# Strassen's seven products for the first channel product of the last two batches

## The chip, the cores and the metric

The kernel runs on one core of a Trainium2 chip, in one launch. The metric is the time of one execution in microseconds, as the median of several runs. The core has five engines that each take their instructions in order: PE (TensorE, matmuls and weight loads), DVE (VectorE), ACT (ScalarE), POOL (GpSimd, here the issuer of most loads) and SP (SyncE, the issuer of stores and of transposing DMAs). They wait for each other through semaphores.

## The reference

Attention with a squared ReLU in place of softmax, for 8 batches, 12 heads, 448 positions and 64 values a head, and a mixer layer on its result:

```python
scores = (q @ k.transpose(0, 1, 3, 2)) / sqrt(64)
attn = maximum(scores, 0) ** 2 / 448
x = (attn @ v).transpose(0, 2, 1, 3).reshape(8, 448, 768)
h = maximum(x.transpose(0, 2, 1) @ w_tok1, 0) @ w_tok2      # 448 -> 256 -> 448, over positions
u = x + h.transpose(0, 2, 1)
out = u + maximum(u @ w_ch1, 0) @ w_ch2                     # 768 -> 1536 -> 768, over channels
```

Inputs and output are float32; the kernel multiplies in bfloat16 and accumulates in float32.

## The kernel before, in words

The work is cut into 24 super-steps `s` of four heads, three to a batch. For each there are, by the names that stand in the code and in the order:

- `ld{k,q,v}{s}.{half}`: loads, cast to bfloat16 on the way, issued by POOL (L274). `kqT` is then made either by PE (`T{s}`, L379, with the copies `cp`, for the first ten super-steps) or by a transposing DMA: VectorE copies `k` and `q` into the one buffer `side` (`ik`, `iq`, L398), SP issues the transpose (`xk`, `xq`, L402).
- `S{s}.{c}`, seven score products (L420), each four matmuls of 64 rows and 64 columns that share the array; `r{s}.{c}.{e}`, their two evictions with the ReLU (L252 on ScalarE or L254 on VectorE), into one of ten buffers `sq`; `q{s}.{c}`, the square, on VectorE (L427).
- `V{s}.{c}`, the products with `v` (L444), again 64 x 64; `xe`, their evictions (L454, L456); `X`/`xc` or `xd`, the transpose of the result, by PE or by DMA (L467).
- `t1`, `rt`, `t2`, `u`: the token products (L488, L497) and the addition of `x` into `uT` (L501). `ub{b}.{g}` transposes `uT` back to `u_sb` by DMA (L513).

For each batch `b` there are twelve chunks of the first channel product, `C1.{b}.{e}` (L533): six matmuls of 128 x 128 weights from `wc1` and 448 columns of `uT`, accumulated in one PSUM bank and evicted with the ReLU to `r2` by `c1e{b}.{e}`. `r2` and `u_sb` are rings of eleven blocks of 128 rows.

The second channel product already goes by Strassen's seven products, over pairs `p` of row blocks: `P1.{p}` to `P7.{p}` (L584), six matmuls each, on weights summed once at the start (`ws`, L317) and on sums of `r2` (`s1` to `s4`, L571). Products that enter two outputs are accumulated in one bank and read out in between: `a`, `b`, `c` and `f21` (L599) add `u_sb` and write an output block, `f11`, `f12`, `f22` (L601) add to what is there. `st` are the stores (L633).

The order of all engines is one list, `ORDER`, written out in the file: each word is an operation, with the PSUM banks for a PE operation (`S0.2:23`) and the engine for an eviction (`:A` ScalarE, `:D` VectorE). `fill:2*13` is 13 matmuls with no use but to keep PE running. An engine executes its operations in the list's order; there is no scheduler behind it.

`ident`, the unit matrix for PE's transposes, is made by POOL. It stands behind nine loads in POOL's queue.

Of the kernel before, what the change touches and what calls it, by code (L numbers as in the profile page):

```python
# [6 lines left out]
FP32 = mybir.dt.float32  # L7
# [8 lines left out]
NSUM = 6  # L16

# [43 lines left out]
ldf.1 ldk0.0 ldf.0 ldk0.1 ldq3.1 ldk2.1 ldq1.0 ldq1.1 cast1.0:A cast1.1:D ldk1.0 ldk1.1 ldv0.1 cast0.0:D cast0.1:A  # L61
ident ldv0.0 T0.0:0 T0.1:1 ldq2.0 cp0.0:A cp0.1:D ldk2.0 fill:2*13 S0.2:23 ldq2.1 S0.5:45 S0.3:67 r0.2.0:A r0.2.1:D
S0.4:10 ldv1.1 r0.3.1:A r0.5.0:D r0.3.0:A ldk3.0 r0.5.1:D T1.0:23 r0.4.1:A ldq3.0 q0.2:D S0.1:74 r0.4.0:A ldv1.0
cp1.1:D cp1.0:A r0.1.0:D ldv2.1 r0.1.1:A fill:5*19 S1.1:65 q0.3:D ldq4.1 S0.0:01 S1.0:32 r1.1.1:A S1.2:74 q0.1:D
r0.0.0:A ldk3.1 r0.0.1:D r1.2.1:A ldv2.0 r1.2.0:D r1.0.1:A r1.0.0:A q0.0:D wc1.0 r1.1.0:A q0.4:D V0.0:50 S1.3:14
wt1.1 q0.5:D V0.1 r1.3.0:A V0.2 r1.3.1:D S1.6:72 wt1.0 V0.3 S0.6:36 q1.0:D V0.4 r1.6.1:A ldk4.0 r0.6.1:D V0.5
r0.6.0:A T2.0:14 ldq4.0 r1.6.0:A q1.1:D cp2.1:A ldk4.1 cp2.0:D q0.6:D wt2 q1.2:D fill:2*24 V0.6 S1.5:26 S1.4:37
q1.3:D ldv3.1 xe0.0:A S2.4:14 r1.5.0:A r1.5.1:D xe0.1:A r1.4.1:D r1.4.0:A X0.1:5 q1.5:D V1.0:26 xc0.1:A S2.2:07
q1.4:D V1.1 r2.2.1:A r2.2.0:D V1.2 T3.0:35 r2.4.0:A q1.6:D r2.4.1:A S2.1:70 V1.3 cp3.0:D cp3.1:A V1.4 r2.1.1:D V1.5
r2.1.0:A q2.2:D V1.6 S2.0:14 S2.5:35 xe1.0:A q2.1:D S3.2:07 r2.0.0:A r2.0.1:D r2.5.0:A ldv3.0 r2.5.1:D xe1.1:A  # L70
q2.0:D r3.2.0:A ldk6.1 r3.2.1:A q2.4:D V2.0:21 S2.3:43 S3.1:56 q2.5:D V2.1 r2.3.1:A ldv4.1 S2.6:07 r2.3.0:D V2.2
r3.1.0:A ldk5.0 r2.6.1:D r2.6.0:A S3.5:34 X1.1:5 r3.1.1:A q2.3:D ldk5.1 r3.5.1:A q2.6:D ldq6.0 fill:0*9 V2.3
r3.5.0:A S3.0:07 xc1.1:D S3.4:64 V2.4 r3.0.0:A r3.0.1:D X1.0:3 ldk6.0 r3.4.1:A X0.0:5 q3.1:D V2.5 xc1.0:A S3.3:07
ldq5.0 xc0.0:D V2.6 r3.4.0:A q3.0:D t1.0.1:4 ldq5.1 xe2.0:A xe2.1:D T4.0:35 rt0.1:A ldv4.0 r3.3.1:D r3.3.0:A X2.0:6
X2.1:2 cp4.1:A q3.2:D t1.0.0:1 ldv5.0 t1.1.0:4 cp4.0:D rt0.0:A ldq6.1 t1.1.1:0 xc2.0:A xc2.1:D rt1.0:D S3.6:75 wc1.1
# [631 lines left out]
```

## Time and profile before

| | |
|---|---|
| median of 3 runs | 364.04 us (363.62 to 365.6) |
| the profiled execution | 361.52 us |
| its span, first to last instruction | 359.7 us |
| PE busy | 342.2 us, 95% |
| VectorE busy | 296.4 us, 82% |
| ScalarE busy | 192.4 us, 53% |
| POOL busy | 92.1 us, 26% |
| granted TensorE clock | 0.994 |

Times in the profile are microseconds from the first instruction of one profiled execution. A busy PE is not PE at its peak, since a matmul's record holds its latency and matmuls overlap: rates are read from the length of a run of matmuls. A group's line gives the count, the busy time, the mean of one in ns, and the idle time ahead of them with what ended it.

### The profile page before, as it was taken

What the parts mean: (1) busy time and instruction counts of PE and PEld (TensorE: products, weight loads), DVE (VectorE), ACT (ScalarE), POOL (GpSimd) and SP (SyncE); (2) the same over time, 40 slices, a digit from 0 to 9 for tenths busy, and PEclk for the clock granted to TensorE, in tenths of its full rate; (3) what the DMA queues carried; (4) which work ended last, traced back from release to release, by engine and by line L of the source; (5) the groups of instructions that cost most, each with busy time, mean ns of one, the idle gap of its engine ahead of it and who ended that gap; (6) DMA issues with size and microseconds to landing.
All of it is one profiled execution on the core that took longest, in us unless ns stands there. A gap on an engine that the chain in (4) does not pass through costs nothing.

```text
span 359.7 us, 8735 instructions
## 1 busy us (share of the span) xinstructions
PE 342.2 (95%) x3494; PEld 190.6 (53%) x3494; DVE 296.4 (82%) x568; ACT 192.4 (53%) x407; POOL 92.1 (26%) x157
## 2 busy tenths in 40 slices
PE   5787999999999999999999999799999999999994
PEld 3565555455546545555545555355455555555562
DVE  1899999998899998999799999699999954165283
ACT  3789987764862187831776155464777322431300
POOL 8847533056054230640203071110300000000000
PEclk9899999999999999999999999999999999999999
DMA  8999999569999999999699999974794221631435
GB/s 153 168 196 173 156 202 202 102 98 163 169 154 179 143 175 183 175 183 138 95 210 144 172 130 161 236 123 84 122 162 108 56 41 29 157 76 23 104 105 158
DMA packets 100505, 50.42 MB, mean 140 GB/s; under 512 B 72880, under 2 KB 97136, under 8 KB 100464
## 3 DMA queue, kind: packets, MB, share of 16 engines
q0 software_dynamic: 25904, 21.47, 44.1%
q1 hardware_dynamic: 74240, 28.00, 43.4%
q8 instruction: 27, 0.44, 0.5%
q10 hardware_dynamic: 320, 0.39, 0.3%
q14 instruction: 14, 0.11, 0.1%
HBM read 43.38 MB, written 11.01 MB: 151 GB/s over the span
## 4 chain that ended last, share of the span: by engine, by line
PE 80%; DMA 8%; issue 5%; DVE 3%; POOL 3%; DVEq 0%; POOLq 0%
PE m_ps L533 27%; PE m_ps L584 25%; PE sc_ps L420 8%; PE acc_ps L444 8%; PE t_ps L488 6%; PE h_ps L497 5%; DMA kqT<-side 4%; DMA v_raw<-in_v_dram 2%; DMA k_raw<-in_k_dram 2%; POOL k_raw L274 1%; PE kqT_ps L379 1%; DVE sq L427 1%; DVE sq L254 1%; POOL v_raw L274 1%; PE x_ps L479 1%
## 5 line engine op out<-in xcount | busy, mean ns | idle before, releaser
L252 ACT ACTIVATE sq<-sc_ps 128x448 bf16<-128x448 f32 x213 | 102.5, 554 | 38.7 <-PE sc_ps L420 37.5
L533 PE MATMUL m_ps<-uT_sb,wc 128*128 128x448 bf16 x576 | 118.5, 353 | 0.0
L427 DVE TENSOR_TENSOR sq<-sq 128x896 bf16<-128x896 bf16 x168 | 97.2, 619 | 0.2
L252 ACT ACTIVATE r_sb<-m_ps 128x448 bf16<-128x448 f32 (+3 forms) x115 | 51.6, 471 | 70.1 <-PE m_ps L533 69.8
L533 PEld LDWEIGHTS <-wc 128*128 128x128 bf16 x576 | 54.1, 98 | 54.6 <-issue 9.0
L254 DVE TENSOR_SCALAR sq<-sc_ps 128x448 bf16<-128x448 f32 x123 | 71.3, 618 | 6.6 <-PE sc_ps L420 6.4
L444 PE MATMUL acc_ps<-sq,v_raw 64*64 64x448 bf16 x672 | 56.7, 354 | 4.4 <-DVE sq L427 2.4
L420 PE MATMUL sc_ps<-kqT 64*64 64x448 bf16 x672 | 57.9, 356 | 2.8 <-DVE xT L456 1.7
L274 POOL DMA_DIRECT2D v_raw<-in_v_dram x48 | 29.4, 615 | 78.7 <-PE acc_ps L444 62.7
L274 POOL DMA_DIRECT2D k_raw<-in_k_dram x48 | 29.5, 621 | 72.2 <-DVE side L398 44.2
L584 PEld LDWEIGHTS <-r_sb 128*128 128x128 bf16 x336 | 32.5, 98 | 24.0 <-issue 1.6
L599 DVE TENSOR_TENSOR out_sb<-m_ps,u_sb 128x384 f32<-128x384 f32 x56 | 30.8, 553 | 11.7 <-PE m_ps L584 11.3
L420 PEld LDWEIGHTS <-kqT 64*64 64x64 bf16 x672 | 22.9, 106 | 20.4 <-issue 12.9
L584 PEld LDWEIGHTS <-sums 128*128 128x128 bf16 x252 | 24.3, 98 | 17.4 <-issue 0.4
L444 PEld LDWEIGHTS <-v_raw 64*64 64x64 bf16 x672 | 20.5, 106 | 21.7 <-issue 14.4
L274 POOL DMA_DIRECT2D q_raw<-in_q_dram x46 | 28.3, 626 | 11.9 <-DVE side L398 11.2
L584 PE MATMUL m_ps<-wc,r_sb 128*128 128x384 bf16 x168 | 31.3, 326 | 0.0
L501 DVE TENSOR_TENSOR uT_sb<-h_ps,xT 128x448 bf16<-128x448 f32 x48 | 28.8, 617 | 3.0 <-PE h_ps L497 3.0
L584 PE MATMUL m_ps<-wc_t,r_sb 128*128 128x384 bf16 x168 | 30.7, 326 | 0.2 <-DVE out_sb L599 0.2
L584 PE MATMUL m_ps<-wc_t,sums 128*128 128x384 bf16 x168 | 30.8, 326 | 0.0
L601 DVE TENSOR_TENSOR out_sb<-m_ps,out_sb 128x384 f32<-128x384 f32 x42 | 23.0, 553 | 8.4 <-PE m_ps L584 8.1
L252 ACT ACTIVATE r_sb<-t_ps 128x512 bf16<-128x512 f32 (+1 forms) x25 | 13.9, 559 | 26.2 <-PE t_ps L488 26.2
(49 smaller groups left out, 246.6 us busy)
## 6 DMA issues: line engine op xcount, KB each, us to landing
out_dram<-out_sb SPq DMA_DIRECT2D x52, 192.0 KB, 3.1
k_raw<-in_k_dram POOLq DMA_DIRECT2D x48, 112.0 KB, 5.2
v_raw<-in_v_dram POOLq DMA_DIRECT2D x48, 112.0 KB, 5.2
q_raw<-in_q_dram POOLq DMA_DIRECT2D x46, 112.0 KB, 5.1
wc<-in_moe_w_ch_dram POOLq DMA_DIRECT2D x2, 1152.0 KB, 10.6
wc<-in_moe_w_ch_dram POOLq DMA_DIRECT2D x3, 576.0 KB, 9.1
u_sb<-uT_sb SPq DMA_TRANSPOSE x60, 3.2
sums<-in_moe_w_ch_dram POOLq DMA_DIRECT2D x1, 576.0 KB, 14.7
```

Of the source, the lines that this page charges most:

```text
L252: nc.scalar.activation(out, ps, AF.Relu)
L254: nc.vector.tensor_scalar(out=out, in0=ps, scalar1=0.0, scalar2=None, op0=ALU.max)
L274: nc.gpsimd.dma_start(out=raws[t][s % NR[t]][64 * half:64 * (half + 1)], in_=src[b, h0:h0 + 2].rearrange('e (p c) d -> p e (c d)', c=KC))
L420: nc.tensor.matmul(o.ps[e][64 * half:64 * (half + 1), :S], lhsT=lhsT, rhs=rhs, start=True, stop=True, skip_group_check=True)
L427: sq_ops[s, c] = [add(Op(f'q{s}.{c}', 'DVE', lambda o: nc.vector.tensor_tensor(out=buf, in0=buf, in1=buf, op=ALU.mult), ev))]
L444: nc.tensor.matmul(o.ps[half][64 * e:64 * (e + 1), :S], lhsT=r[rows, e, c * D:(c + 1) * D], rhs=sq[rows, e, :], start=c == 0, stop=c == KC ...
L488: nc.tensor.matmul(o.ps[:, j, :], lhsT=wt1[:, c, j * 128:(j + 1) * 128], rhs=x_sb[:, p0:p1, c, :], start=c == 0, stop=c == 3)
L501: nc.vector.tensor_tensor(out=uTs[bb % 2][:, 2 * i + a, off:off + S].rearrange('n (c p) -> n c p', c=KC), in0=t2.ps[:, :S].rearrange('n (p ...
L533: nc.tensor.matmul(ps[:, :S], lhsT=wc1[:, g, e * 128:(e + 1) * 128], rhs=uT[:, g, off:off + S], start=g == 0, stop=g == CC - 1)
L584: nc.tensor.matmul(banks[into][:, :HN], lhsT=lhs[:, e], rhs=wc2[w][:, e], start=after is None and e == 0, stop=e == EH - 1, skip_group_che ...
L599: nc.vector.tensor_tensor(out=out_[:, cols].rearrange('n (g d) -> n g d', d=128), in0=banks[into][:, :HN].rearrange('n (g d) -> n g d', d= ...
L601: nc.vector.tensor_tensor(out=out_[:, cols], in0=banks[into][:, :HN], in1=out_[:, cols], op=ALU.add)
```

## The change

The first channel product of batches 6 and 7 is computed for both together (`PAIRED = 2`). The two batches are the two column halves of one matrix, the two halves of the 768 inputs its row halves, and `wc1` is a 2 x 2 matrix of halves of inputs and outputs. Seven products of half size, `Q1` to `Q7`, for each of six blocks `k` of 128 outputs, three matmuls each, take the place of 2 x 12 chunks of six matmuls. With them come

- `y1` to `y4`, sums of the weights, in two halves each, on VectorE; three of them go to the buffers of `k` and `q` once the last super-steps have left them, one over a quarter of `wc1`;
- `m1` to `m4`, sums of the inputs, in two parts each, on VectorE; they go to `sq` buffers, `m3` over a part of `uT`;
- `na`, `nb`, `nc`: float32 snapshots of the accumulating bank, in `sq` buffers (most on ScalarE);
- `h11`, `h12`, `h22`: VectorE adds a bank and a snapshot into `r2`, without the ReLU; `h21` evicts with the ReLU;
- `g1`, `g2`: the ReLU in place on `r2`.

Batch 6 lies over the end of the ring `r2`, so its writes are two pieces, of 128 and 320 columns. To make the buffers adjacent, the `k` and `q` buffers become one tile, and the `sq` buffers one. The whole of `ORDER` is another list; it also splits evictions between ScalarE and VectorE in other places, loads `wc1` later, and has `ident` behind seven loads instead of nine, and the second half of the first transposes ahead of the first.

```diff
+PAIRED = 2
 ORDER = """
-ldf.1 ldk0.0 ldf.0 ldk0.1 ldq3.1 ldk2.1 ldq1.0 ldq1.1 cast1.0:A cast1.1:D ldk1.0 ldk1.1 ldv0.1 cast0.0:D cast0.1:A
-ident ldv0.0 T0.0:0 T0.1:1 ldq2.0 cp0.0:A cp0.1:D ldk2.0 fill:2*13 S0.2:23 ldq2.1 S0.5:45 S0.3:67 r0.2.0:A r0.2.1:D
...
+ldf.1 ldk0.1 ldf.0 ldk0.0 ldq1.1 ldk1.0 ldk1.1 ldq1.0 cast1.0:A cast1.1:D ldv0.0 ident cast0.0:D cast0.1:A ldv0.1
+T0.1:0 T0.0:1 ldk2.1 cp0.1:A cp0.0:D ldq2.0 fill:2*13 S0.6:23 ldk2.0 S0.4:45 S0.1:67 r0.6.0:A r0.6.1:D S0.0:10
...
+h11.1:D Q7.1 ub6.0 h22.0:D Q5.1:3 g2.0:D na.2:A Q3.0 h11.2:D Q6.2 h12.0:D Q4.0 nb.2:A ub6.4 nc.1:D P5.9:6 g1.0:A
+h21.0:D Q1.3:4 h22.1:D P4.9 f22.9:D na.3:A g2.1:D Q3.1 f21.9:D Q1.4:2 h12.1:D st19.0 Q2.3:1 ub7.4 g1.1:A Q7.2
...
+h12.4:D Q4.4 g1.4:D nc.5:A Q2.5:1 st19.1 h21.4:A h22.5:D P1.10:0 h11.5:D g2.5:A Q3.5 a.10:D Q4.5 h12.5:D P2.10:7
+h21.5:A g1.5:D s1.10:D P1.11:4 s1.11:D s2.10:D P5.10:5 a.11:D s2.11:D P6.10 s3.11:D s3.10:D P6.11 b.10:D s4.10:D
...
 """
...
-    raws = {t: [sbuf.tile([128, 2, KC * D], BF16, name=f'{t}_raw{i}') for i in range(NR[t])] for t in 'kqv'}
+    kq_raw = sbuf.tile([128, NR['k'] + NR['q'], 2, KC * D], BF16, name='kq_raw')
...
-    sqs = [sbuf.tile([128, 2, S], BF16, name=f'sq{i}') for i in range(NSQ)]
+    sq_all = sbuf.tile([128, NSQ, 2, S], BF16, name='sq')
+    sqs = [sq_all[:, i] for i in range(NSQ)]
+    GH = CC // 2
+    spare = kq_raw.rearrange('p i e d -> p (i e d)')[:, :3 * GH * HC].rearrange('p (w g n) -> p w g n', w=3, g=GH)
+    wsq = {1: spare[:, 0], 2: spare[:, 1], 4: spare[:, 2], 3: wc1[:, :GH, HC:]}
...
+    snaps = [sq_all[:, 6 + i].rearrange('p e n -> p (e n)').bitcast(FP32) for i in range(4)]
...
+    def channel1_pair(b):
...
+        B = {(i, j): uT[:, (low, high)[i], j * S:(j + 1) * S] for i in range(2) for j in range(2)}
+        A = {(i, j): wc1[:, (low, high)[j], i * HC:(i + 1) * HC] for i in range(2) for j in range(2)}
...
+            for w, x, y, op in ((1, A[1, 0], A[1, 1], ALU.add), (2, wsq[1], A[0, 0], ALU.subtract), (3, A[0, 0], A[1, 0], ALU.subtract), (4, A[0, 1], wsq[2], ALU.subtract)):
...
+        for w, x, y, i, j in ((1, B[0, 1], B[0, 0], (0, 1), (0, 0)), (2, B[1, 1], usum[1], (1, 1), None), (3, B[1, 1], B[0, 1], (1, 1), (0, 1)), (4, B[1, 0], usum[2], (1, 0), None)):
...
+        for k in range(EH):
...
+                    for g in range(GH):
+                        nc.tensor.matmul(banks[into][:, :S], lhsT=lhs[:, g, k * 128:(k + 1) * 128], rhs=rhs[:, g], start=after is None and g == 0, stop=g == GH - 1, skip_group_check=True)
...
+                    for x, y, to in pieces[a]:
+                        out_, ps = (r2[:, e, to:to + y - x], banks[into][:, x:y])
+                        if z is None:
+                            relu(o, out_, ps)
+                        else:
+                            nc.vector.tensor_tensor(out=out_, in0=ps, in1=snaps[bufs[z]][:, x:y], op=ALU.add)
...
+                    for a, b_ in parts:
+                        relu(o, r2[:, e, a:b_], r2[:, e, a:b_])
...
+            q1 = product(1, A[0, 0], B[0, 0], ins[0, 0] + ([ue[NS - 1, 1]] if k else []), 'x', end='h21')
+            na = snap('a', q1)
+            q6 = product(6, wsq[2], usum[2], wd(2) + td(2), 'x', na)
+            nb = snap('b', q6)
+            q7 = product(7, wsq[3], usum[3], wd(3) + td(3), 'x', nb)
+            nc_ = snap('c', q7)
+            q4 = product(4, A[1, 1], usum[4], td(4), 'x', nc_)
+            h21 = write('h21', 0, k + EH, None, [q4], 'x')
+            q2 = product(2, A[0, 1], B[1, 0], ins[1, 0] + [q1], 'y', end='h11')
+            h11 = write('h11', 0, k, 'a', [q2, na], 'y')
+            q5 = product(5, wsq[1], usum[1], wd(1) + td(1) + [q1], 'z', end='h12')
+            h22 = write('h22', 1, k + EH, 'c', [q5, nc_], 'z')
+            q3 = product(3, wsq[4], B[1, 1], wd(4) + ins[1, 1], 'z', h22)
+            h12 = write('h12', 1, k, 'b', [q3, nb], 'z')
...
+            g1 = relu_row('g1', both, k, [h11, h12])
+            g2 = relu_row('g2', row2, k + EH, [h22])
...
     for b in range(B):
-        for e in range(EC):
-            channel1(b, e, b == 0 and e < PARTIAL)
+        if b < B - PAIRED:
+            for e in range(EC):
+                channel1(b, e, b == 0 and e < PARTIAL)
+        elif b % 2 == 0:
+            channel1_pair(b)
```

More of the change, by code (lines that the diff above doesn't have):

```diff
@@ L66 @@
[L66 to L75, printed above, removed]
@@ L215 @@
     EH = EC // 2
+    HC = DC // 2
     RT = RING * 128
```

333 lines of the change are left out of this document (209 added, 124 removed).

## The prediction

> **What bounds the kernel now.** I read the page's busy times first, then the table of equal stretches, then the chain that ended last, then the groups of instructions by shape.
>
> ```profile
> span 359.7 us, 8735 instructions
> ...
> PE 342.2 (95%) x3494; PEld 190.6 (53%) x3494; DVE 296.4 (82%) x568; ACT 192.4 (53%) x407; POOL 92.1 (26%) x157
> ```
>
> ```profile
> core 0: us, PE busy (x) PEld busy (x) DVE busy (x) ACT busy (x) POOL busy (x), PEclk, DMA share, GB/s
> 0.00:10.00 10.00, 6.19 (x78) 3.80 (x78) 2.26 (x8) 3.35 (x4) 8.88 (x20) 0.88 0.89 156
> 10.00:20.00 10.00, 7.70 (x219) 5.78 (x218) 8.99 (x17) 8.45 (x18) 9.04 (x15) 0.95 1.15 171
> 20.00:30.00 10.00, 6.54 (x155) 4.18 (x156) 10.00 (x20) 8.36 (x18) 4.26 (x9) 1.00 1.24 200
> 30.00:40.00 10.00, 9.98 (x211) 6.45 (x199) 10.00 (x21) 9.97 (x23) 7.18 (x11) 1.00 1.03 143
> ...
> 90.00:100.00 10.00, 9.15 (x167) 5.05 (x165) 8.30 (x16) 7.89 (x16) 0.00 (x0) 1.00 1.24 168
> ...
> 220.00:230.00 10.00, 8.29 (x82) 3.90 (x81) 6.70 (x14) 4.90 (x12) 1.77 (x3) 1.00 1.30 192
> ...
> 240.00:250.00 10.00, 10.00 (x96) 5.49 (x94) 10.00 (x21) 4.83 (x11) 0.00 (x0) 1.00 0.42 82
> ...
> 300.00:310.00 10.00, 10.00 (x61) 5.81 (x60) 4.01 (x7) 2.72 (x8) 0.00 (x0) 1.00 0.44 106
> ```
>
> Three regimes show. Up to 30 us PE waits and VectorE and ScalarE are nearly full: the evictions of the first scores set the pace. From 30 us PE is full, except in two stretches (90 to 100, 220 to 230) in which VectorE has holes too. Until attention ends VectorE is almost as full (10.00 of 10 at 240); after it VectorE is below half (4.01 at 300).
>
> The chain of waits, in order of time, shows the issue times; "x12" is the number of matmuls in a piece.
>
> ```profile
> 124.29 0.57 PE acc_ps L444 x12
> ...
> 133.51 0.69 PE sc_ps L420 x12
> ...
> 284.14 0.69 PE acc_ps L444 x12
> 284.83 1.24 PE h_ps L497 x6
> ...
> 305.07 0.87 PE t_ps L488 x8
> ...
> 332.18 6.81 PE m_ps L533 x36
> 338.99 15.61 PE m_ps L584 x96
> 354.63 0.56 DVE out_sb L601
> ```
>
> A matmul of the first channel product takes 6.81 / 36 = 0.189 us, so a chunk of six 1.135; one of the second takes 15.61 / 96 = 0.163, a product of six 0.976. The last attention product ends at 284.83. Behind it the order holds 24 chunks `C1`, 39 products `P`, 2 `t1` (0.87) and 7 `t2` (1.24 / 3 = 0.41): 27.2 + 38.1 + 1.7 + 2.9 = 69.9 us, and 284.83 + 69.9 = 354.7, where the last PE piece ends (354.60). So the last 70 us hold no PE stall at all: a matmul removed there is time removed, if nothing else gets late.
>
> [...]
>
> **The change, part by part.** The sum is made against the profiled execution, 361.52 us with a span of 359.7. The median of the runs shown is 364.04, 2.52 more; I add that at the end.
>
> *Products.* Two batches took 24 x 6 = 144 matmuls; now 7 products x 6 blocks x 3 = 126. 18 x 0.189 = **-3.4 us** of PE.
>
> *Where PE's work stands.* The new order has 70 `C1` and 55 `P` up to the end of attention, where the old one has 72 and 59: 2 x 1.135 + 4 x 0.976 = 6.2 us go from the attention stage to the tail. The tail is then 2 `C1`, 43 `P`, 126 small products, the same `t1` and `t2`: 2.3 + 42.0 + 23.8 + 4.6 = 72.7 us instead of 69.9. So attention has to end 2.8 us earlier merely to come out even; the gain of 3.4 is had only if the 6.2 show up before 284.83.
>
> *Changes between the 64-row and the full form.* Twelve 64-row matmuls take 0.57 us in the row at 124.29 and 0.69 in that at 133.51, ahead of a full matmul: 0.12 for a change. The written PE order has 129 changes, was 119: 10 x 0.12 = **+1.2**, bounds 0 and 1.2 (a change in a stall costs nothing).
>
> *The start.*
>
> ```profile
> 2.54 0.62 POOL L274 DMA_DIRECT2D q_raw<-in_q_dram  x1
> ...
> 6.76 0.58 ACT L258 ACTIVATE q_raw<-side 64x448 bf16<-64x448 f32 x1 [2.15 <-DMA side<-in_q_dram]
> ...
> 7.00 0.32 POOL masks.py:199 TENSOR_SCALAR_AFFINE_SELECT ident<-ident 128x128 bf16<-128x128 bf16 x1
> ...
> 7.38 0.48 PE L379 MATMUL kqT_ps<-ident,k_raw 64*64 64x64 bf16 x14 [2.62 <-POOL ident masks.py:199]
> ```
>
> `ident` stands behind seven loads on POOL instead of nine: 2 x 0.62 = 1.24 earlier, at 6.08. The half whose query was cast first is now transposed first and needn't wait; the other half still needs the cast that ends at 6.76 + 0.58 = 7.34. One of the two half transposes is hidden, about half of the time from 7.38 to the fill matmuls at 8.72: **-0.7**, bounds 0 and -1.2. The two loads that are moved past it are needed only for later super-steps.
>
> *Up to the first channel product* PE waits for evictions. Ahead of it the new order gives VectorE 3 squares and 4 score evictions less (0.58 each, prices in the fence below) and 2 `xc` more (0.42), -3.2 us, and ScalarE, on balance, about 0.7 more; -2.5 over two engines is up to -1.2 us, and more (-2.0) if the `v` load that PE waited for also comes sooner, because the weight loads `wc1` are issued later. I take **-0.6**, bounds 0 and -2.0, since ScalarE was at 9.97 of 10 already.
>
> *VectorE in the attention stage.*
>
> ```profile
> L427 DVE TENSOR_TENSOR sq<-sq 128x896 bf16<-128x896 bf16 x168 | 97.2, 619 | 0.2
> L254 DVE TENSOR_SCALAR sq<-sc_ps 128x448 bf16<-128x448 f32 x123 | 71.3, 618 | 6.6 <-PE sc_ps L420 6.4
> L252 ACT ACTIVATE r_sb<-m_ps 128x448 bf16<-128x448 f32 x69 | 37.6, 547 | 51.9 <-PE m_ps L533 51.6
> L601 DVE TENSOR_TENSOR out_sb<-m_ps,out_sb 128x384 f32<-128x384 f32 x42 | 23.0, 553 | 8.4 <-PE m_ps L584 8.1
> L398 DVE COPY side<-k_raw 128x896 bf16<-128x896 bf16 x14 | 8.6, 612 | 3.3 <-DMA kqT<-side 2.8 <-DMA k_raw<-in_k_dram 0.4
> L571 DVE TENSOR_TENSOR sums<-r_sb 128x768 bf16<-128x768 bf16 x14 | 7.6, 552 | 15.1 <-ACT r_sb L252 15.1
> L456 DVE TENSOR_SCALAR xT<-acc_ps 128x448 bf16<-128x448 f32 x12 | 7.4, 616 | 0.0
> L317 DVE TENSOR_TENSOR wc_t<-wc,wc_t 128x1152 bf16<-128x1152 bf16 x4 | 2.8, 756 | 0.0
> L260 DVE COPY x_sb<-x_ps 128x512 bf16<-128x512 bf16 x3 | 1.3, 420 | 0.0
> L254 DVE TENSOR_SCALAR r_sb<-m_ps 128x384 bf16<-128x384 f32 x1 | 0.5, 547 | 0.0
> L254 DVE TENSOR_SCALAR r_sb<-m_ps 128x64 bf16<-128x64 f32 x1 | 0.2, 217 | 0.0
> ```
>
> The order gives VectorE 112 score evictions instead of 123 (71.3 / 123 = 0.58 each), 5 sums `s` fewer (0.55) and 2 additions to the output fewer (0.55), but 3 `xe` more (0.62), 3 `xc` more (0.42) and six of the eight weight sums `y`, which have the shape of L317 (0.756): -6.4 - 2.8 - 1.1 + 1.9 + 1.3 + 4.5 = -2.6. PE's work there falls by 6.2 - 1.2 = 5.0. Both must fall for the stage to shorten. From 30 to 280 us VectorE was busy for 235.69 of 250:
>
> ```profile
> 30.00:280.00 250.00, 247.14 (x2587) 134.50 (x2576) 235.69 (x449) 153.62 (x324) 69.90 (x116) 1.00 1.03 154
> ```
>
> So 14.3 us of holes are there, and 5.0 can be had if 2.4 of them close. I charge **+0.5** for it, bounds 0 and +2.4 (5.0 - 2.6: no hole is given up).
>
> *The pair's evictions, in the tail.* New on VectorE, by the same fence. From 64 to 384 columns a PSUM eviction goes from 217 to 547 ns, 1.03 ns a column on 151: pieces of 128 and 320 are 0.28 + 0.48. So six `h11` and one `h21` 0.76 each, twelve `h12` and `h22` and two snapshots 0.62, the input sums `m` 4 x (0.62 + 0.38). For the relu passes over `r2`, from SBUF to SBUF, the trace has no row; the nearest are the copy L398, 896 columns in 0.612, and L571: 448 columns 0.38, 128 + 768 columns 0.21 + 0.55. Above, the price of a PSUM eviction: 0.62 and 0.28 + 0.94. Between the last `t2` and the first sum of pair 10, PE has 29 us of products and VectorE 7 x 0.76 + 14 x 0.62 + 7 x 0.55 + 1.6 + 4 x 0.76 + 5 x 0.38 = 24.4, or 27.5 by the upper price. It fits, closely: an eviction that comes late holds a PSUM bank that the next product wants (bank 3 goes from `Q2.4` to `Q1.5` with 2.8 us of products between). Snapshots on ScalarE (16 x 0.55) find it idle. **+0.5**, bounds 0 and +4.
>
> [...]
>
> *The end.*
>
> ```profile
> out_dram<-out_sb SPq DMA_DIRECT2D x52, 192.0 KB, 3.1
> ...
> kqT<-side SPq DMA_TRANSPOSE x28, 4.5
> ...
> out_dram<-out_sb SPq DMA_DIRECT2D x4, 96.0 KB, 2.2
> ```
>
> The last stores are halves of a row block, 2.2 us, where whole ones, 3.1, ended it: **-0.5**, bounds 0 and -0.9.
>
> *The waits at 90 and 220 us.*
>
> ```profile
> 227.82 0.62 DVE L398 COPY side<-k_raw 128x896 bf16<-128x896 bf16 x1 [2.83 <-DMA kqT<-side]
> ...
> 229.02 0.57 PE L420 MATMUL sc_ps<-kqT 64*64 64x448 bf16 x7 [1.65 <-DVE xT L456]
> ```
>
> VectorE's copy into the one buffer `side` waits for the transposing DMA of the super-step before; evictions queue behind it, and PE stops: 1.65 us here, 0.85 (10.00 - 9.15) at 90. What decides is the PE work between that DMA's place in the order and the next copy, against 4.5 us to landing. The old order has 3.5, 3.8 and 4.6 us as its tightest; the new one 3.8 and 4.0 (super-step 19), then 5.0. The same number of tight places: **0**, bounds -2.5 (none stalls) and +5.
>
> Sum: -3.4 + 1.2 - 0.7 - 0.6 + 0.5 + 0.5 - 0.5 + 0 = **-3.0 us**: 358.5 profiled, 361.0 as a median. A measurement of this kernel tells about 0.5% (1.8 us) from no change, so faster means under 362.2, slower over 365.9.
>
> **The rivals.**
>
> A. *VectorE sets the length of attention.* The 10.00 of 10 at 240 speaks for it, its holes against it. Then that stage shortens by 2.6 instead of 5.0, and the start's 0.6 is lost: -3.0 + 2.4 + 0.6 = 0, 364.0.
>
> B. *The copies into `side` stall more often (the slower end).* The place is attention from super-step 10 on; a stall costs 1.65 us, as at 229. The new order puts the pairs of transposes close together, and they share SP's queue with the transposes `xd` and `ub`, so they may land later than 4.5. From three further stalls on it decides: -3.0 + 5.0 = +2.0, four +3.6: 367. Against it: the old order, as tight, had two.
>
> C. *The stalls go and the first stage gives its bound.* -3.0 - 2.5 - 1.4 = -6.9: 357.1. Two tight places speak against it.
>
> D. *The pair waits for its evictions.* At the upper price VectorE has 27.5 of 29 us, and half a microsecond in each of the six blocks gives -3.0 + 3 = 0: 364.0. The zero stalls of the old tail speak against it.
>
> That the products don't get fewer is excluded: the built order holds 126 matmuls in their place.
>
> **How the numbers follow.** Forecast 0.46, with its own range 359 to 363 (faster 0.40, within 0.06); A 0.14 and D 0.10 (within); B 0.17 (slower); C 0.13 (faster). Within is 0.06 + 0.14 + 0.10 = 0.30, faster 0.53, slower 0.17. The range goes from C's 357.0 to B's 367.0; left out are half of C and half of B, and a tail of both.
>
> **What would show it.** Right: the last attention product ends about 279 us, the tail from there to the last PE piece is near 73 us with no stall over half a microsecond, VectorE stays under 9.5 of 10 in it, the first transposes start near 6.1. Wrong: attention ends after 282 us with PE below 10.00 in its stretches (A, or B where the copy into `side` is what waited); holes of PE in the pair's blocks with evictions queued (D).

## The result, and the profile after

The changed kernel took 362.44 us as the median of 20 runs (355.52 to 370.54); the kernel before 363.14 (20 runs, 360.85 to 366.73). The ratio given with them, 0.9868 (95% interval 0.9828 to 0.9909), leaves out every run more than 1.5% above the fastest of its kernel, and with the changed kernel's fastest far out at 355.52 that is 14 of its 20; a second set, with 12 runs of the changed kernel, gives 0.9994 (0.9958 to 1.0031) and medians of 363.69 and 362.69. So I go by the medians of all runs: 0.7 us less in one set and 1.0 more in the other, no change that this measurement can tell. What did change is the spread: over the 32 runs of the changed kernel the standard deviation is 3.2 us, over 100 of the kernel before 1.4.

The profiled execution took 362.15 us. Its page, busy times:

```profile
span 360.3 us, 8771 instructions
...
PE 343.7 (95%) x3486; PEld 188.4 (52%) x3486; DVE 317.5 (88%) x621; ACT 193.7 (54%) x406; POOL 92.6 (26%) x157
```

By stretches, in the columns of before:

```profile
0.00:10.00 10.00, 7.18 (x94) 4.22 (x98) 2.85 (x10) 4.14 (x6) 8.88 (x20) 0.89 0.87 150
10.00:20.00 10.00, 9.62 (x239) 6.99 (x233) 9.76 (x19) 9.57 (x21) 8.88 (x15) 0.94 1.19 177
20.00:30.00 10.00, 8.94 (x227) 5.44 (x224) 10.00 (x20) 9.81 (x21) 6.12 (x10) 1.00 1.02 139
30.00:40.00 10.00, 10.00 (x188) 6.17 (x189) 9.96 (x21) 9.93 (x25) 4.66 (x8) 1.00 1.08 169
90.00:100.00 10.00, 9.94 (x83) 5.56 (x82) 9.90 (x20) 5.50 (x12) 2.38 (x4) 1.00 1.22 178
200.00:210.00 10.00, 6.17 (x31) 3.47 (x30) 4.23 (x9) 2.65 (x6) 3.76 (x7) 0.83 1.34 151
...
300.00:310.00 10.00, 10.00 (x57) 5.46 (x56) 7.58 (x18) 2.25 (x5) 0.00 (x0) 1.00 0.20 43
...
330.00:340.00 10.00, 10.00 (x64) 6.05 (x62) 9.12 (x19) 0.00 (x0) 0.00 (x0) 1.00 0.01 3
```

PE is much fuller from 10 to 30 us (9.62 and 8.94, were 7.70 and 6.54), and full in the tail, where VectorE now has 7.58 and 9.12 of 10. But from 200 to 210 it has 6.17: a stretch that was nearly full before (9.81).

The chain and the timeline place the ends of the stages (time, duration, what):

```profile
6.42 0.97 PE L391 MATMUL kqT_ps<-ident,kq_raw 64*64 64x64 bf16 x56 [1.57 <-POOL ident masks.py:199]
...
8.58 1.34 PE L432 MATMUL sc_ps<-kqT 64*64 64x448 bf16 x12
...
40.88 1.31 PE L545 MATMUL m_ps<-uT_sb,wc 128*128 128x448 bf16 x6 [0.47 <-DMA wc<-in_moe_w_ch_dram]
```

```profile
282.02 0.88 PE acc_ps L456 x16
282.91 0.48 PE h_ps L509 x2
...
329.36 26.34 PE m_ps L710 x162
```

The first channel product starts at 40.88 (before: 44.59), the last attention product ends at 282.9 (before 284.8), and the tail from there to the last PE piece is 329.36 + 26.34 - 282.90 = 72.8 us. PE's waits between the first channel product and the end of attention, first of before, then of the changed kernel (waiting line, what it waited for: us in total, times, longest):

```profile
PE sc_ps L420 <- DVE xT L456: 1.7, 1, 1.7
PE sc_ps L420 <- DVE sq L254: 0.8, 1, 0.8
...
```

```profile
PE t_ps L500 <- DMA x_sb<-xT: 3.8, 1, 3.8
PE m_ps L710 <- DVE out_sb L725: 1.3, 1, 1.3
PE acc_ps L456 <- DVE sq L439: 0.9, 1, 0.9
PE m_ps L710 <- DVE out_sb L727: 0.5, 1, 0.5
PE m_ps L545 <- DMA wc<-in_moe_w_ch_dram: 0.5, 1, 0.5
...
```

The longest is a token product that waits for its transposing DMA. The next two, at 162.4 and 145.8 us, come from the other two kinds of transpose, as the chain of waits shows: an output block needs `u_sb`, whose transpose `ub` took 7.11 us to land, and the copy into `side` needs the transpose ahead of it, which took 5.30:

```profile
140.52 5.30 DMA kqT<-side
...
145.84 0.62 DVE side L410
...
147.04 0.38 PE acc_ps L456 x4
...
156.21 7.11 DMA u_sb<-uT_sb
```

Around the longest, in order of time:

```profile
196.05 0.59 POOL L286 DMA_DIRECT2D v_raw<-in_v_dram  x1 [8.46 <-PE acc_ps L456]
196.48 1.54 SPq L479 DMA_TRANSPOSE x_sb<-xT  x1
196.63 0.60 POOL L286 DMA_DIRECT2D kq_raw<-in_q_dram  x1
197.22 0.61 POOL L286 DMA_DIRECT2D v_raw<-in_v_dram  x1
197.80 0.62 POOL L286 DMA_DIRECT2D kq_raw<-in_k_dram  x1
198.38 0.63 POOL L286 DMA_DIRECT2D kq_raw<-in_q_dram  x1
198.70 4.01 SPq L525 DMA_TRANSPOSE u_sb<-uT_sb  x2
198.97 1.83 POOL L286 DMA_DIRECT2D kq_raw<-in_k_dram  x3
...
205.80 1.89 PE L500 MATMUL t_ps<-x_sb,wt 128*128 128x256 bf16 x8 [3.83 <-DMA x_sb<-xT]
```

POOL stands for 8.46 us at a load whose buffer PE has not yet left; seven loads whose buffers are free wait behind it. Then eight go out within 4 us, and the transpose that SP issues at 196.48 lets PE go on only 9.3 us later, at 205.80. This row became the theory of the study.

**One table for all kernels.** From the start times of the matmuls in each profiled execution: the start of the first channel product; the attention stage from there to the start of the last attention matmul; the PE waits in it (wherever the next matmul starts over 0.45 us after the one before, less 0.12); the rest; the same at full clock, an estimate that takes off half of the time in which PE worked at a granted clock of 0.50; the tail to the start of the last matmul, its waits in brackets.

| kernel | first C1 | attention | waits | without them | at full clock | tail | span |
|---|---|---|---|---|---|---|---|
| before | 44.59 | 239.9 | 3.8 | 236.1 | 236.1 | 69.8 | 359.7 |
| changed | 40.88 | 241.7 | 8.3 | 233.4 | 231.7 | 72.8 | 360.3 |
| after_again | 40.03 | 240.0 | 8.2 | 231.7 | 231.7 | 72.8 | 357.8 |
| ident_late | 41.99 | 240.5 | 8.8 | 231.7 | 230.4 | 72.8 | 360.3 |
| pair_only | 46.07 | 243.1 | 6.0 | 237.1 | 235.7 | 69.5 (3.1) | 363.7 |
| order_only | 40.04 | 241.9 | 9.1 | 232.8 | 231.1 | 77.3 (1.3) | 364.6 |
| three_early | 41.40 | 246.6 | 14.7 | 231.9 | 230.5 | 72.8 | 365.7 |
| after_loads | 41.08 | 241.8 | 10.0 | 231.8 | 230.3 | 72.6 | 360.4 |
| after_both | 40.52 | 244.8 | 11.7 | 233.2 | 230.4 | 72.6 | 362.8 |
| before_both | 45.06 | 247.8 | 10.3 | 237.6 | 236.1 | 69.8 | 368.1 |
| one_load | 41.71 | 237.2 | 5.5 | 231.8 | 230.3 | 72.8 | 356.7 |
| after_paced | 43.26 | 235.1 | 4.9 | 230.2 | 230.2 | 72.6 | 355.9 |
| before_paced | 45.56 | 245.8 | 8.1 | 237.7 | 236.0 | 69.8 | 366.6 |
| after_paced2 | 41.18 | 235.3 | 4.7 | 230.6 | 230.6 | 72.6 | 354.0 |

Without its waits the attention stage has nearly one length for each order of PE's work, whatever the queues do: 236.1 to 237.7 in the old order, 230.2 to 233.4 in the new; at full clock 235.7 to 236.1, and 230.2 to 231.7. What differs from kernel to kernel is the waits and, behind some of them, the clock (last section).

### The profile page after: what moved, and what is told of

The parts are those of the page before. It is cut to its first block, busy times and chain, and to the rows that moved or that the text cites. A ratio compares the mean times of both kernels' runs of the same rounds, so it can differ in the third digit from the quotient of the medians.

```text
span 360.3 us, 8771 instructions
## 1 busy us (share of the span) xinstructions
PE 343.7 (95%) x3486; PEld 188.4 (52%) x3486; DVE 317.5 (88%) x621; ACT 193.7 (54%) x406; POOL 92.6 (26%) x157
## 4 chain that ended last, share of the span: by engine, by line
PE 70%; DMA 11%; DVE 10%; SPq 3%; ACT 2%; issue 2%; POOL 2%; DVEq 0%; ACTq 0%; POOLq 0%
PE m_ps L710 21%; PE m_ps L545 18%; PE sc_ps L432 7%; PE acc_ps L456 7%; PE m_ps L617 6%; PE t_ps L500 5%; PE h_ps L509 4%; DVE sq L439 3%; DMA u_sb<-uT_sb 3%; DMA wc<-in_moe_w_ch_dram 3%; DMA x_sb<-xT 3%; SPq L525 2%; DMA kqT<-side 1%; ACT sq L264 1%; DVE out_sb L727 1%
## 5 line engine op out<-in xcount | busy, mean ns | idle before, releaser
L264 ACT ACTIVATE sq<-sc_ps 128x448 bf16<-128x448 f32 x224 | 109.0, 561 | 19.4 <-PE sc_ps L432 18.7
L545 PE MATMUL m_ps<-uT_sb,wc 128*128 128x448 bf16 x432 | 89.8, 353 | 0.5 <-DMA wc<-in_moe_w_ch_dram 0.5
L266 DVE TENSOR_SCALAR sq<-sc_ps 128x448 bf16<-128x448 f32 x112 | 65.5, 615 | 4.2 <-PE sc_ps L432 3.7
L264 ACT ACTIVATE r_sb<-m_ps 128x448 bf16<-128x448 f32 (+2 forms) x88 | 40.7, 481 | 47.8 <-PE m_ps L545 46.3
L545 PEld LDWEIGHTS <-wc 128*128 128x128 bf16 x432 | 40.3, 98 | 42.4 <-issue 7.2
L456 PE MATMUL acc_ps<-sq,v_raw 64*64 64x448 bf16 x672 | 55.6, 354 | 1.0 <-DVE sq L439 0.9
L286 POOL DMA_DIRECT2D kq_raw<-in_q_dram x46 | 28.6, 624 | 56.3 <-DVE side L410 32.9
L286 POOL DMA_DIRECT2D kq_raw<-in_k_dram x48 | 29.8, 631 | 19.0 <-DVE side L410 16.0
L710 PE MATMUL m_ps<-wc_t,sums 128*128 128x384 bf16 x168 | 31.9, 332 | 0.1
L500 PE MATMUL t_ps<-x_sb,wt 128*128 128x256 bf16 (+1 forms) x216 | 26.0, 266 | 3.8 <-DMA x_sb<-xT 3.8
```

Source lines behind the costliest of these rows:

```text
L264: nc.scalar.activation(out, ps, AF.Relu)
L266: nc.vector.tensor_scalar(out=out, in0=ps, scalar1=0.0, scalar2=None, op0=ALU.max)
L286: nc.gpsimd.dma_start(out=raws[t][s % NR[t]][64 * half:64 * (half + 1)], in_=src[b, h0:h0 + 2].rearrange('e (p c) d -> p e (c d)', c=KC))
L456: nc.tensor.matmul(o.ps[half][64 * e:64 * (e + 1), :S], lhsT=r[rows, e, c * D:(c + 1) * D], rhs=sq[rows, e, :], start=c == 0, stop=c == KC ...
L500: nc.tensor.matmul(o.ps[:, j, :], lhsT=wt1[:, c, j * 128:(j + 1) * 128], rhs=x_sb[:, p0:p1, c, :], start=c == 0, stop=c == 3)
L545: nc.tensor.matmul(ps[:, :S], lhsT=wc1[:, g, e * 128:(e + 1) * 128], rhs=uT[:, g, off:off + S], start=g == 0, stop=g == CC - 1)
```

## The experiments

The theory (1): the change gains what its parts say, and loses it in attention where PE waits for transposing DMAs that land late. The rival (2): VectorE sets the pace of attention, and the waits are only where its lateness shows.

### The parts of the change

**after_again** is the changed kernel, unaltered.

> The changed kernel once more, unaltered, for a second profiled execution. Theory 1 (a steady gain, part of it given back in attention where PE waits for transposing DMAs that land late): the median is 356 to 360 us where the execution has few such waits; in its profile the first channel product starts near 40.9 us and the tail behind the last attention product is 72.7 us again, while the stalls stand in other places than 145.8, 162.4 and 201.7 us, or are shorter, so that attention ends up to 5 us earlier than 282.7. Theory 2 (VectorE sets the pace of attention): the stalls and the end of attention are the same to 0.5 us.

363.69 us (12 runs, 359.53 to 367.18; the profiled one 359.53). The tail is 72.8 again and the first channel product starts at 40.03. The waits are again 8.2 us, partly in the same places (145.5, 168.4, 200.8), with other lengths: 2.3 instead of 4.2 us at 201, and a new one of 2.1 at 206.7. The end of attention came 2.5 us earlier: 0.85 of it from the first stage, and 1.7 from attention without waits, where the changed kernel's first profile has a stretch at half clock and this one has none. The median missed theory 1's 356 to 360 us, and its places held more often than it said; theory 2's "the same to 0.5 us" failed too. The same 8 us of waits in both executions speak for a systematic loss of which only the size at each place varies.

**ident_late** undoes the start of the new order:

```diff
-ldv0.0 ident cast0.0:D cast0.1:A ldv0.1 T0.1:0 T0.0:1 ldk2.1
+ldv0.0 cast0.0:D cast0.1:A ldv0.1 ldk2.1 ident T0.0:1 T0.1:0
```

> The changed kernel with the unit matrix behind nine loads again and the first half of the first transposes ahead of the second; all else as changed. Theory 1: the first transposes start 1.0 us later (7.4 instead of 6.4), the first scores up to 1.8 later, and since PE is full behind the first stage the end is 0.7 to 1.8 us later than the changed kernel's. Theory 2: evictions set the pace up to 40 us, so the first channel product starts at the same time and nothing is lost (within 0.3 us).

362.71 us (12 runs, 359.32 to 366.46). The transposes start at 7.40 instead of 6.2 to 6.4, the scores at 10.22 instead of 8.1 to 8.6, the first channel product at 41.99 instead of 40.0 to 40.9. The 1 us at the transposes is shown. What is left of it at the first channel product is not: in the kernels below whose beginning is the changed one's, the scores start at 8.5 to 9.6 and that product at 40.5 to 43.3. The run time doesn't show it either (0.9985 of before, 0.9947 to 1.0023; 1.0 us under the changed kernel's median in the same set), so theory 1's loss of 0.7 to 1.8 us did not show.

**pair_only** is the old order up to the last attention product (with `y1` and `y2` put between and `y4` behind it), then the changed kernel's tail.

> The kernel before up to the last attention product, with four of the weight sums put between, and then the changed kernel's tail with the seven products: the products without the new order of attention. Theory 1: 18 matmuls of 0.189 us less, so 3.4 us less than before, ratio 0.990 to 0.993 with up to 0.9 us lost where the weight sums delay evictions. Theory 2 (the gain is the new order's alone): within 1 us of before. Theory 3 (the pair waits for its evictions): slower than before by 1 us or more, with PE holes behind 310 us.

364.03 us (12 runs, 361.79 to 366.06), ratio to before 1.0061 (1.0034 to 1.0087): no theory's number. The products do what was said: the tail is 69.5, of which 3.1 are waits, so 66.4, 3.4 less than before's 69.8. The waits are my splice's. In the chain:

```profile
290.74 0.55 ACT xT L461
291.29 0.01 issue
291.30 3.22 DMA x_sb<-xT
294.51 0.05 issue
294.56 1.05 PE t_ps L495 x8
```

A token product is placed there before its transpose can have landed. The rest is 1.0 us in attention without waits, 2.2 in its waits, and 1.5 in a later first channel product, ahead of which nothing in the order was changed. The 1.0 need not be the weight sums: the granted clock was 0.50 for 3.4 us behind a wait of 2.24 us at 229.5, which is up to 1.7 us, and at full clock the stage is 0.4 us shorter than before's. Why the first channel product came later is not shown; the stretch of half clock that before has from 7.6 us stands here from 30.4.

**order_only** is the new order without the weight sums up to the last attention product, then twelve chunks each for batches 6 and 7.

> The changed kernel's order up to the last attention product without the weight sums, and then twelve chunks each for batches 6 and 7 as before: the new order without the seven products. Theory 1: the first channel product starts 3.7 us earlier than before (40.9 instead of 44.6), and of that up to 2 us are given back in attention: 1.5 to 3.5 us less than before. Theory 2 (the gain is the products' alone): within 0.7 us of before. The two single parts should add up to the whole gain of about 4.8 us within 1 us if they don't act on each other.

367.55 us (6 runs, 366.15 to 371.32), ratio 1.0173 (1.012 to 1.0225): theory 1 had the sign wrong, theory 2 the size, and the parts don't add up (+1.3 and +4.9 against about 0). The table says why: the new order begins 4.5 us earlier (40.04), but it carries 6.2 us of work into the tail (77.3) and takes only 3.3 us less for attention without waits (232.8; 5.0 less at full clock), where it waits 9.1 us instead of 3.8. Here -4.5 + 2.0 + 7.5 = +5.0. The seven products then take 3.1 off the tail (75.9 without its wait, against 72.8): from order_only to the changed kernel in the same set of runs, -3.9.

### The late transposes

**three_early** moves three transposes forward in SP's queue, two of which had landed within 0.12 us of their readers: `ub2.5` behind `ub2.2`; `xd14`, `ub3.5` ahead of `st8.0`.

> The changed kernel with three transposing DMAs issued earlier in SP's queue and nothing else moved: ub2.5 (its input ready near 120 us, issued at 155, landed 0.1 us ahead of its reader), xd14 ahead of five stores and of xk18, xd15 and xq18 (ready near 182, issued at 195, landed 0.05 us ahead of its reader) and ub3.5 behind it (ready at 172, issued at 197). Theory 1 (the gain is lost where PE waits for these three): the PE waits near 162 to 168, 201 and 207 us, 5 to 6 us together, go, and the kernel is 3 to 6 us faster than the changed one, ratio to the kernel before 0.985 to 0.993. Theory 2 (attention is paced by VectorE or by the DMA engines as a whole): the waits come back in other places and the time is within 1 us of the changed kernel's.

366.5 us (12 runs, 361.55 to 371.19), 3.3 above the median of the kernel before in the same set, with a ratio of 1.0026 (0.9985 to 1.0067): none of the 3 to 6 us that theory 1 wanted. The profiled execution, one of the longer ones at 367.47, shows what took their place:

```profile
196.52 0.59 POOL L281 DMA_DIRECT2D v_raw<-in_v_dram  x1 [8.46 <-PE acc_ps L451]
...
198.23 1.50 SPq L409 DMA_TRANSPOSE kqT<-side  x1
...
199.43 1.83 POOL L281 DMA_DIRECT2D kq_raw<-in_k_dram  x3
...
208.75 1.33 PE L427 MATMUL sc_ps<-kqT 64*64 64x448 bf16 x12 [9.05 <-DMA kqT<-side]
```

`xd14` now lands in 3.9 us and `ub3.5` in 5.1, for they are issued at 186 to 188. But `xq18`, which they pushed back, is now the one that SP issues into the same burst of loads: 198.23 to 208.62, 10.4 us to landing, and PE stands for 9.05. The victim changed, the burst stayed, and its price rose. That speaks against "late by their place" alone, and against theory 2: PE and VectorE both stand idle there (0.00 and 0.43 us of work from 200 to 208).

**after_loads**: from 70 us on POOL's loads in the order in which their buffers come free; SP's queue as changed.

> The changed kernel with POOL's loads from 70 us on issued in the order in which their buffers come free, instead of the order written, in which a load whose buffer is still in use holds up 5 to 8 others that then go out in one burst. Theory 1a (the transposes land late because of the bursts): the median landing of x_sb falls from 5.1 us towards 4, that of kqT from 5.5 below 5, the PE waits near 145, 201 and 207 us shrink by over half without any change in SP's queue, 3 to 6 us faster than the changed kernel. Theory 1b (they are late because they are issued late, behind stores in SP's queue): landings get shorter by under 1 us, the waits stay, under 1.5 us gained.

363.72 us (12 runs, 361.06 to 374.53), ratio 1.0017 (0.9979 to 1.0056): nothing gained. Near 201 and 207 us, where now only four loads stand in place of thirteen, `xd14` and `ub3.5` land in 5.9 and 3.6 us (were 7.7 and 10.6; `ub3.5` from its first piece's issue) and the waits shrink from 4.4 to 3.3. But the loads, sooner issued, form another burst: six from 138.4 to 141.4, where the changed kernel's second profile has none from 133 to 143.8; `xk14`, issued at 140.63, takes 10.0 us, VectorE's copy into `side` waits for `kqT`, and PE's longest wait is now there:

```profile
150.71 0.62 DVE L405 COPY side<-kq_raw 128x896 bf16<-128x896 bf16 x1 [5.07 <-DMA kqT<-side]
...
151.91 1.65 PE L451 MATMUL acc_ps<-sq,v_raw 64*64 64x448 bf16 x13 [4.22 <-DVE sq L261]
```

A second place where a burst makes a wait: 1a's mechanism, not its forecast.

**after_both** and **before_both** add SP's transposes and stores in the order of need, to the changed kernel and to the kernel before.

> The changed kernel with POOL's loads in the order in which their buffers come free and SP's transposes and stores, from 70 to 265 us, in the order of who needs them first among those that are ready; PE, VectorE and ScalarE keep the changed kernel's order. Theory 1: attention loses nearly all of its 8 us of PE waits, so the last attention product starts near 274 instead of 280 to 282.5 and the kernel takes 354 to 358 us. Theory 2 (VectorE paces): the last attention product stays within 2 us of 280.

> The kernel before with the same two rules for POOL's loads and SP's queue. Its PE waits were 3.8 us in the profiled execution, at 98.6 and 227 us. Theory 1: up to 3 us faster than the kernel before, that is 359 to 362 us, so that the changed kernel under the same rules keeps 3 to 6 us on it: the change's own gain once its queues don't spoil it. Theory 2 (the change is worth nothing by itself): the two kernels under the same rules are within 1 us.

after_both 364.06 us (12 runs, 357.4 to 371.94), before_both 369.04 (6 runs, 365.3 to 370.36; ratio 1.0139, 1.0089 to 1.0188). Both expectations failed: the waits in attention rose to 11.7 and 10.3 us. In after_both 12 loads go out from 75.8 to 82.4 us, SP issues transposes one behind another from 80 on, and those up to 96 take 10 to 11.7 us to land (`xd6` 10.1, `ub0.3` 11.7); PE lost 5.9 us at 99. Issuing everything as early as it is ready brought more waits in both orders: 11.7 us where the changed kernel has 8.3, and 10.3 where the kernel before has 3.8.

**one_load** moves one word, the load that blocks POOL at 186 to 195 us, behind the seven that wait for it:

```diff
-ldv19.1 ldq22.1 ldv17.1 ldk22.0 ldq20.0 ldk20.0 ldk22.1 ldk21.0 ldv19.0
+ldq22.1 ldv17.1 ldk22.0 ldq20.0 ldk20.0 ldk22.1 ldk21.0 ldv19.1 ldv19.0
```

> The changed kernel with one load moved: ldv19.1, which waits near 186 to 195 us for the last product of super-step 16 while seven loads with free buffers stand behind it, goes behind those seven. So they are issued from 186 us instead of in one burst from 195.8. Theory 1a (bursts of loads make the transposes land late): xd14 and ub3.5, issued near 195 and 197 us, land in 3 to 5 us instead of 7.7 and 10.6; the PE waits near 201 and 207 us, 4.4 us together in the second profile of the changed kernel, fall below 1.5; 2 to 4 us faster than the changed kernel if nothing else gets worse. Theory 1b (they are late by their place in SP's queue): landings as before, nothing gained.

365.86 us (6 runs: two at 358.52 and 359.54, four at 365.27 to 372.22), no better; the profiled one was the fastest of them. In it the burst stands at 185.7 to 189.9, `xd14` and `ub3.5` land in 6.5 and 6.1 us and no longer hold PE, and `xq18`, issued at 192.85, does for 2.6. The landings lie between those of 1a and 1b. The burst that was moved found another victim, though with 5.5 us of waits this execution is shorter than either of the changed kernel's; what the longer runs waited for, no trace shows.

**after_paced** has no bursts. From 64 us on one load is issued every 2 us, the earliest needed among those with free buffers; each is given a wait for the PE instruction that starts at about its time.

```diff
+GATE = dict((x.split(":") for x in """
+...
+""".split()))
...
-                nc.gpsimd.dma_start(out=raws[t][s % NR[t]][64 * half:64 * (half + 1)], ...)
+                x = nc.gpsimd.dma_start(out=raws[t][s % NR[t]][64 * half:64 * (half + 1)], ...)
+                if o.name in GATE:
+                    tc.add_manual_dep(x.ins, plan.ops[GATE[o.name]].last.ins.name, ...)
```

> The changed kernel with the loads from 64 us on spread evenly: one every 2 us, those first whose buffers are free and which are needed first; each waits for a PE instruction that starts at about its time. All other queues as changed. Theory 1a: no bursts, so the landings of the transposes have medians below 4 us for x_sb and 4.5 for kqT, PE waits in attention fall from 8 us to under 4, the last attention product starts near 276 instead of 280 to 282.5, and the kernel takes 356 to 359 us, under both kernels. Theory 2 (VectorE paces attention): the end of attention stays at 280 or later.

356.58 us (6 runs, 353.06 to 358.85), ratio to before 0.9804 (0.9753 to 0.9855). The time is 1a's; the last attention product starts at 278.4 (1a said 276, theory 2 no earlier than 280), with 4.9 us of waits (1a said under 4). Theory 2 is out, since VectorE's work is untouched. POOL's loads have nearly the order of after_loads (a load is 1.4 places from its place there on average, at most 8), and all other engines have the same; so what parts 363.72 from 356.58 us is in the main the spacing. PE's waits in attention, and the landings (median us from issue):

```profile
PE acc_ps L270 <- DVE sq L453: 2.6, 1, 2.6
PE sc_ps L270 <- DMA kqT<-side: 1.8, 1, 1.8
PE m_ps L270 <- DMA wc<-in_moe_w_ch_dram: 1.4, 1, 1.4
```

```profile
u_sb<-uT_sb SPq DMA_TRANSPOSE x60, 3.3
kqT<-side SPq DMA_TRANSPOSE x28, 4.4
x_sb<-xT SPq DMA_TRANSPOSE x19, 5.2
```

`kqT` fell from 5.1 and 5.5 to 4.4 as expected, `x_sb` stayed at 5.2 (5.5 and 5.1 in the changed kernel, expected below 4): the medians hardly move, the long ones do. No transpose that SP issues from 185 to 200 us takes over 7.8 us (9.1 and 10.0 in the two profiles of the changed kernel). From 70 to 265 us 4 of 84 take over 7 us; in the changed kernel's profiles 33 of 166 do, in after_loads 19 of 82.

**before_paced** spreads the loads of the kernel before by the same rule.

> The kernel before with its loads spread by the same rule. Its PE waits in attention are 3.8 us in the profiled execution. Theory 1a: up to 2.5 us faster than the kernel before, 360 to 363 us; then the changed kernel is 3 to 5 us faster under the same rule, which is what the earlier start and the 18 matmuls are worth. Theory 2 (the change is worth nothing by itself): the two kernels with spread loads are within 1 us.

367.79 us (6 runs, 367.11 to 370.1), ratio 1.0147 (1.0112 to 1.0182): slower, which no theory said. Its waits are 8.1 us instead of 3.8, with 4.2 at 198 where PE waits for `x_sb`. So even spacing is no gain by itself; the 11 us between the two paced kernels are not the change's worth. Why it hurts the old order is open. That `x_sb` was issued at 193.09 and took 9.0 us to land with loads 1.5 to 2.4 us apart, behind four stores that SP issued from 189.9: a late landing without a burst of loads.

**after_paced2** moves `xq18` directly behind `xk18` in SP's queue, and VectorE's copy `iq15` with `xq15` behind two squares and an eviction.

> The changed kernel with the spread loads and two more places mended, at which its profile showed PE waits: xq18 goes directly behind xk18 in SP's queue, ahead of three stores, ub4.0 and xd15 (it waited 7.6 us there and landed 0.14 us ahead of its reader), and VectorE's copy iq15 with its transpose xq15 goes behind two squares and an eviction of scores (it held them up for 3.07 us until xq14 had landed). Theory 1a: the waits near 147 us (3.0) and 198.5 us (2.2) fall below 1 us each; 2 to 4 us faster than the kernel with spread loads alone, 352.5 to 355. Rival: as in the kernel with three transposes moved, another transpose behind these becomes the late one, and the time stays at 356 to 358.

355.76 us (6 runs, 351.6 to 359.0), ratio to before 0.973 (0.9666 to 0.9794). The wait near 198 is gone (0.7 at 200.8 is left), that near 147 is 2.7 instead of 3.0; the waits sum to 4.7, and the time, just above 1a's 352.5 to 355, can't be told from after_paced. Either version is under both kernels: by 6.4 and 8.5 us under the kernel before in its own set of runs, by 6 to 7 under the changed kernel's median of 362.8 over its 32 runs, which stand in other sets.

## Why the prediction was right, and where not

The profiled time was forecast at 358.5, the median at 361.0; they were 362.15 and 362.4 to 363.7. The time lies in the range and the kernel can't be told from the one before, as the range allowed; the gain of 3.0 us did not come. That the median ended within 1.4 to 2.7 us of the forecast is luck in part: the waits cost 4.5 us where the sum had nothing, and the front gave 2.4 more than it had. By its own signs the profiled execution is one of the wrong ones in attention, which ended at 282.9 instead of about 279, and a right one in the tail. Its steps, against the kernel before in the profiled executions:

- **Products, -3.4: shown.** 3.4 in pair_only's tail, 3.1 between order_only and the changed kernel, waits taken out.
- **The tail of 72.7 us without a stall: shown**, 72.6 to 72.8 in every profiled execution of that order; the largest hole is 0.42 us at 315.
- **Form changes +1.2 and VectorE +0.5, with 6.2 us moved out of attention:** 236.1 - 6.2 + 1.2 + 0.5 = 231.6; without waits the stage has 230.2 to 233.4 in the nine profiled executions with the changed order on PE and VectorE's work as changed, 231.7 to 231.9 in five of them. So the sum fits, but some of it is the clock: at full clock the changed kernel's own two have 231.7, which is the two charges paid in full, and the other seven 230.2 to 230.6, where 0.3 to 0.7 of the 1.7 us were paid. The two terms weren't measured apart.
- **Start and first stage, -1.3: mis-sized.** The first channel product starts 3.7 us earlier; by the table 40.0 to 43.3 in the new order, 44.6 to 46.1 in the old. That is more than the two bounds together (-3.2); ident_late, with the old start, still has 2.6 of it, so most comes from the stage behind the first transposes. I took ScalarE's 9.97 of 10 from 30 to 40 us as a sign that there was no room, but PE waited from 10 to 30, where ScalarE had 8.45 and 8.36; it has 9.57 and 9.81 now.
- **The pair's evictions, +0.5: about 0**, and rival D is out. VectorE was cheaper than the row I took for the passes of the ReLU over `r2`. Groups of the tail by shape:

```profile
L266 DVE TENSOR_SCALAR r_sb<-r_sb 128x768 bf16<-128x768 bf16 x4 | 1.4, 359 | 0.0
L266 DVE TENSOR_SCALAR r_sb<-r_sb 128x448 bf16<-128x448 bf16 x5 | 1.4, 275 | 0.1
...
L266 DVE TENSOR_SCALAR r_sb<-r_sb 128x128 bf16<-128x128 bf16 x4 | 0.7, 185 | 0.0
```

From 128 to 768 columns 174 ns, 0.27 ns a column, a quarter of the 1.03 of a PSUM eviction: nine passes take 3.6 us, where I had 4.9.
- **The end, -0.5: shown**: 4.99 us from the last matmul's start to the end of the span, was 5.47.
- **The waits, 0 with bounds -2.5 and +5: the step that failed.** They are 8.3 us, were 3.8: +4.5. I had looked at one kind, the copy into `side`, and counted the PE work ahead of it against the median landing of the kernel before. That median itself rose, from 4.5 to 5.1 and 5.5 us for `kqT` and from 3.9 to 5.5 and 5.1 for `x_sb`, and PE waited for all three kinds of transpose: 4.0 us at 201.6 for `x_sb` (9.3 us to landing) and 1.6 at 162.4 for `u_sb` (7.1), both issued into bursts of loads, and 1.2 at 145.8 behind the copy into `side`, where `kqT` took 5.3 us and no load had been issued from 133 to 144. The diff moved POOL's loads, and their order was in the list I had; I read POOL's queue only at the start. So rival B was right in direction, and in place for the last of these waits alone; and the 3.7 us at the front hid it in the sum: -3.7 (start) + 1.8 (attention: -4.4 at full clock, +1.7 by the half clock behind the longest wait, for which the sum had no term, and +4.5 in the waits) + 3.0 (tail) - 0.5 (end) = +0.6, which is 360.3 - 359.7.
- **Rival A** (VectorE sets attention): against it after_paced and after_paced2, with the same work on VectorE and an end of attention 1.6 to 6.1 us earlier than in the changed kernel's two profiles. **Rival C**: the first stage gave its bound and more, but the stalls grew.

What stays open: why landings differ so much between two executions of one kernel, and why spread loads slow the old order. That the bursts cause late landings is shown at three places (199, 147 and 80 to 100 us), each time by moving loads; that nothing else does is not, and before_paced has one without a burst. In the third the transposes' own number was raised too. All fourteen traces together agree: of the 1117 transposes issued from 70 to 265 us whose landing they have, those with at most one load issued from 6 us before to 4 us after land in 3.0 us (median) and none takes over 7, those with eight or more in 7.7, and 62% take over 7. The count of loads goes along with the landing (correlation 0.67), that of stores or of other transposes hardly (0.08 and -0.11).

## What to carry to other kernels

Before a reordering is priced by its engines, go through each DMA queue with three times for every transfer: when its input or buffer is ready, when it is issued, when its reader wants it. Here a load that waited 8.46 us at the head of POOL's queue saved up seven behind it, and a transpose that SP issued into their burst took 9.3 us to land, where the median of its kind was 5.5. Moving the victims forward, or the burst, picked another victim; spreading the loads brought PE's waits in attention from 8.3 to 4.9 us in one order of work, and from 3.8 to 8.1 in the other. And measure a stage's length without its waits beside the waits: here the first stayed within 230.2 to 233.4 us in the new order (at full clock, by the estimate, 230.2 to 231.7), while the waits went from 4.7 to 14.7.

## What the hardware showed that was not expected

A long PE wait can cost more than itself. Behind the wait at 201 us the granted clock (the third column from the right) was 0.50 for 3.4 us:

```profile
200.00:205.70 5.70, 1.97 (x12) 0.98 (x10) 4.23 (x9) 2.05 (x5) 1.99 (x4) 1.00 1.33 141
205.70:209.10 3.40, 3.30 (x14) 1.92 (x15) 0.00 (x0) 0.60 (x1) 1.77 (x3) 0.50 1.38 157
209.10:215.00 5.90, 5.90 (x43) 3.38 (x42) 4.27 (x9) 1.42 (x3) 0.00 (x0) 1.00 1.27 138
```

The second channel product's matmuls start 0.320 us apart from 207.48 to 209.08, and 0.163 from 209.28 on. Half speed for 3.4 us is at most 1.7 us of work lost, besides the wait. Taken off in the table's column "at full clock", it leaves 235.7 to 236.1 us for all four kernels of the old order, which had 236.1 to 237.7, and 230.2 to 230.6 for seven of the nine executions of the new with the weight sums; the changed kernel's own two lie 1.1 to 1.5 us higher, and that is not explained. With the waits taken from one matmul's start to the next, such a stretch came with every wait over 4 us: 4.15 here, 4.22 in before_paced, 4.57 in after_loads, 4.96 in ident_late, 5.91 in after_both (6.8 us long) and 9.41 in three_early (10.2 us long, from 2.5 us into the wait). It also came with waits of 2.2 to 2.6 us in order_only, pair_only, before_both and one_load; it did not with those of 2.96 in after_paced and 3.10 in before_both, nor with eight others between 2.00 and 2.64. The stretches were 3.4 us long, in after_both and three_early two and three times that. The length of a wait alone doesn't decide: behind one of 2.2 us the clock was 0.50, behind one of 3.10 it was 1.00. What does is not shown.
